# Splitting the load of the second x block over two queues, with half of V's weights queued behind the smaller part

## The chip, the cores and the metric

The kernel runs on one core of one Trainium2 chip. The metric is device time in microseconds (us) for one execution; lower is better. A time is the median of several runs. A core has five engines that each work through their own instructions in program order: TensorE (PE in the profile, with its weight loads as PEld), VectorE (DVE), ScalarE (ACT), GpSimd (POOL) and SyncE (SP). SP and ScalarE both issue DMA transfers, each into a queue of its own: q1 is SP's in the profile, q10 ScalarE's.

## The reference

The input x has 2048 rows of 640 values in bf16. Each row is normalized; the normalized x goes through windowed attention with 32 heads of 20 values, and through a gated feed-forward layer with 1536 hidden values. The output is x plus both:

```python
x = A_x
xn = _layernorm(x, axis=-1)
# A: 32 heads, a key is seen from its own row to 255 rows later
qkv = xn @ wqkv                      # 640 -> 3 * 640
p = softmax(mask(q @ k.T * Dh ** -0.5))
A = (p @ v) @ wo
# B: 640 -> 1536 -> 640
B = (sigmoid(xn @ w_gate) * (xn @ w_up)) @ w_down
return x + A + B
```

## The kernel before

The 2048 rows are worked on as four chunks of 512, each chunk as four blocks of 128 rows (128 is the number of partitions). For a chunk the kernel normalizes the blocks, transposes them to `xnT`, projects V (`project_v`, L321), then Q and K (`proj_block`, L294), and goes on to scores, exponentials, the product with V, the gate and up projections and the output. Work of later chunks is put between the attention steps of earlier ones by a list of fillers with costs, so that TensorE always has something to do.

The change is in the first microseconds, before any of that: chunk 0. Its order is written out by hand, and each engine runs its instructions in that order.

Loads. SP issues, one after another: block 0 of x (L171), block 1 (L171), block 3, block 2, the second column half of V's weights (L175), then the weights of Q and K (L165), the first half of the gate and up weights (L197) and two clears of scratch rows (L193). ScalarE issues one load: the first column half of V's weights, 128 partitions x 5 x 320 values, 400 KB (`load_v(0, nc.scalar)`, L179). A block of x is 160 KB, one row of 1280 bytes for each partition. A DMA counts up one of eight semaphores in turn, so that a later DMA that is given the same semaphore waits until the earlier one has landed.

Normalization of chunk 0. Block 0 has its statistics on VectorE (`ln_block`, L247 and L253). Blocks 1 and 3 have theirs on ScalarE: `mean_act` (L598) makes the mean, `root_act` (L603, L604) the variance and its root. The root for block 0 is ScalarE's as well (`root`, L588). The order is the one in which these lines are written:

```python
mv0 = ln_block(0, 0)
xn1, neg1 = mean_act(1)
r0 = root(mv0)
r1 = root_act(1, xn1, neg1)
norm(0, mv0, r0)
for lo, hi in ((0, 3), (3, DC)):
    transpose_rows(0, dve, lo, hi)
v00 = project_v(0, 0, 0)
norm_act(1, xn1, neg1, r1)
```

So on ScalarE the mean of block 1 comes ahead of the root of block 0. VectorE then normalizes block 0 (L592, L267), TensorE transposes it in five pieces (L274), VectorE copies these to `xnT` (L275), and TensorE makes the first product with V's first column half (L321). Block 1 follows in the same way (L608, L609), then both halves of V for blocks 0 to 3, and from there Q and K.

Before that, TensorE runs ten matmuls on constants (`pwarm`, L238), and ScalarE one SQRT on a constant (L234), which loads its function table.

Of the kernel before, what the change touches and what calls it, by code (L numbers as in the profile page):

```python
# [9 lines left out]
P = 128  # L10
# [97 lines left out]
def kernel(  # L108
# [11 lines left out]
    nc = tc.nc  # L120
    x2 = A_x.flatten_outer_dims()
    out2 = out.flatten_outer_dims()
    xr = x2.rearrange("(n p) d -> p n d", p=P)
# [25 lines left out]
    xc = {}  # L149
# [17 lines left out]

    xc[0] = xp.tile([P, SBC, D], BF16, name="xc")

    def load_rows(s, queue):  # L170
        queue.dma_start(out=xc[0][:, s, :], in_=xr[:, s, :])  # L171

    def load_v(hf, queue):
        a = 2 * D + hf * HALF
        queue.dma_start(out=wqkv[:, :, a:a + HALF], in_=wqkv_r[:, :, a:a + HALF])  # L175

    load_rows(0, nc.sync)
    load_rows(1, nc.sync)
    load_v(0, nc.scalar)  # L179
    load_rows(3, nc.sync)  # L180
    load_rows(2, nc.sync)
    load_v(1, nc.sync)
# [601 lines left out]
```

## Time and profile before

| what | value |
|---|---|
| median of 6 runs | 317.11 us (316.17 to 317.8) |
| the profiled execution, its own time | 317.8 us |
| its span, first to last instruction | 316.1 us |
| mean granted TensorE clock over the span | 0.987 |
| first product with V on TensorE (L321) | starts at 7.74 us |
| first product for Q (L294) | starts at 17.66 us |
| bytes that DMA moved in all | 35.71 MB, mean 113 GB/s |

The profile is that of one execution. Its times count from the start of the span. For each engine it lists the busy time and, before an instruction, the idle time and what ended it. "The chain that ended last" is followed back from the last instruction: at each step to what released it, or to the instruction before it on its engine. The granted clock is the share of TensorE's full clock that it was given. In the timeline, lines marked SPq or ACTq are the issues of DMAs by SP and ScalarE.

### The profile page before, as it was taken

The numbers are of one execution on the slowest core, as the hardware profiler recorded it, in microseconds if no ns is written. First come the engines' busy times: TensorE is split into PE (matmuls) and PEld (weight loads), VectorE is DVE, ScalarE is ACT, GpSimd is POOL, SyncE is SP. The second block draws the span as 40 slices with busy tenths as digits, with TensorE's granted clock in tenths as the row PEclk, the third lists the DMA queues.
The fourth block names the chain that finished last, engine by engine and source line by source line (L and its number), as shares of the span: only waits on it lengthen the run. The fifth ranks groups of instructions, "written<-read, shape, count | busy, mean of one in ns | idle before, by whom it ended". The sixth has DMA issues, their size and how long they took to land.

```text
span 316.1 us, 10548 instructions
## 1 busy us (share of the span) xinstructions
PE 308.6 (98%) x4663; PEld 176.7 (56%) x4663; DVE 159.6 (50%) x314; ACT 192.5 (61%) x178; POOL 155.7 (49%) x239
## 2 busy tenths in 40 slices
PE   5999999999999999999999999999999999999995
PEld 2555444556567665654557665654556675444774
DVE  2551746475695445269836245272632526372523
ACT  5424598688864747878574547867575647778000
POOL 3000286666783655748472736636372745556000
PEclk9599999999999999999999999999999999999999
DMA  7956899747554242640026222640000123000002
GB/s 252 372 170 233 264 379 249 221 126 209 177 91 106 64 129 84 198 155 2 4 41 88 66 72 79 206 144 2 2 3 2 62 66 108 0 4 0 5 21 63
DMA packets 37614, 35.71 MB, mean 113 GB/s; under 512 B 10272, under 2 KB 37024, under 8 KB 37536
## 3 DMA queue, kind: packets, MB, share of 16 engines
q1 hardware_dynamic: 36624, 34.51, 37.3%
q8 instruction: 36, 0.59, 0.7%
q10 hardware_dynamic: 944, 0.52, 0.5%
q14 instruction: 10, 0.08, 0.1%
HBM read 23.63 MB, written 10.26 MB: 107 GB/s over the span
## 4 chain that ended last, share of the span: by engine, by line
PE 96%; DMA 1%; DVE 1%; ACT 0%; issue 0%; SPq 0%; DVEq 0%
PE y L421 17%; PE pu L407 17%; PE pg L400 17%; PE pqk L294 14%; PE ps L471 9%; PE pv L321 8%; PE y L428 7%; PE acc L503 7%; DMA xc<-in_A_x_dram 1%; PE pt L274 1%; DVE xnT L275 0%; ACT xn L598 0%; DVE h L411 0%; DVE xn L267 0%; SPq L171 0%
## 5 line engine op out<-in xcount | busy, mean ns | idle before, releaser
L479 POOL TENSOR_SCALAR_AFFINE_SELECT pT<-pT 128x512 bf16<-128x512 bf16 (+2 forms) x192 | 147.2, 798 | 132.6 <-ACT pT L476 132.5
L476 ACT ACTIVATE pT<-ps 128x2048 bf16<-128x2048 f32 x76 | 142.7, 1878 | 64.3 <-PE ps L471 60.4
L411 DVE SCALAR_TENSOR_TENSOR h<-th,pu 128x512 bf16<-128x512 f32 x48 | 32.7, 683 | 60.3 <-PE pu L407 49.2
L407 PE MATMUL pu<-xnT,wu 128*128 128x512 bf16 x240 | 59.8, 380 | 0.0
L400 PE MATMUL pg<-xnT,wg 128*128 128x512 bf16 x240 | 59.8, 380 | 0.0
L421 PE MATMUL y<-wd,h 128*128 128x320 bf16 (+2 forms) x396 | 57.0, 296 | 0.0
L294 PE MATMUL pqk<-xnT,wqkv 128*128 128x512 bf16 x200 | 46.0, 381 | 0.0
L421 PEld LDWEIGHTS <-h 128*128 128x128 bf16 x396 | 36.5, 98 | 14.3
L403 ACT ACTIVATE th<-pg 128x512 f32<-128x512 f32 x48 | 28.6, 596 | 14.5 <-PE pg L400 14.2
L400 PEld LDWEIGHTS <-wg 128*128 128x128 bf16 x240 | 22.3, 98 | 25.3 <-issue 0.2
L407 PEld LDWEIGHTS <-wu 128*128 128x128 bf16 x240 | 21.9, 98 | 25.4 <-issue 0.6
L471 PEld LDWEIGHTS <-kT 20*64 20x64 bf16 x1856 | 20.6, 103 | 24.2 <-issue 21.9
L294 PEld LDWEIGHTS <-wqkv 128*128 128x128 bf16 x200 | 22.5, 119 | 18.0 <-issue 0.6
L471 PE MATMUL ps<-qT,kT 20*64 20x128 bf16 (+4 forms) x1856 | 32.5, 239 | 0.0
L513 DVE STREAM_TRANSPOSE t<-acc 128x512 f32<-128x512 f32 x32 | 22.0, 711 | 18.5 <-PE acc L503 18.2
L432 DVE SCALAR_TENSOR_TENSOR rows<-y,rows 128x320 bf16<-128x320 f32 x30 | 14.5, 490 | 33.2 <-PE y L428 33.1
L525 DVE TENSOR_TENSOR on<-t,rec 128x320 bf16<-128x320 f32 (+4 forms) x48 | 27.6, 574 | 1.1
L321 PE MATMUL pv<-wqkv,xnT 128*128 128x320 bf16 x160 | 26.0, 319 | 0.9 <-DVE xnT L275 0.9
L428 PE MATMUL y<-wo,oc 128*128 128x320 bf16 (+2 forms) x165 | 24.2, 295 | 0.0
L503 PE MATMUL acc<-pT,v 128*32 128x64 bf16 (+3 forms) x1376 | 23.2, 223 | 0.1
L503 PEld LDWEIGHTS <-v 128*32 128x32 bf16 x1376 | 18.6, 97 | 7.9 <-ACT pT L476 1.7
L321 PEld LDWEIGHTS <-xnT 128*128 128x128 bf16 x160 | 15.8, 103 | 8.5 <-DVE xnT L275 1.4
(44 smaller groups left out, 134.0 us busy)
## 6 DMA issues: line engine op xcount, KB each, us to landing
qT<-sq SPq DMA_DIRECT2D x7, 512.0 KB, 6.4
sq<-st SPq DMA_DIRECT2D x20, 128.0 KB, 2.6
sk<-st SPq DMA_DIRECT2D x20, 128.0 KB, 2.9
rows<-in_A_x_dram SPq DMA_DIRECT2D x15, 160.0 KB, 2.2
out_dram<-rows SPq DMA_DIRECT2D x15, 160.0 KB, 1.8
kT<-sk SPq DMA_DIRECT2D x4, 512.0 KB, 6.1
wg<-in_B_w_gate_dram SPq DMA_DIRECT2D x2, 960.0 KB
wu<-in_B_w_up_dram SPq DMA_DIRECT2D x2, 960.0 KB, 9.6
```

The source lines that it names most:

```text
L294: nc.tensor.matmul(ps, lhsT=wt[:, m, :], rhs=xnT[c][:, d, :], start=(d == 0), stop=(d == DC - 1))
L321: nc.tensor.matmul(ps[:, 0:HALF], lhsT=xnT[c][:, d, s * P:(s + 1) * P], rhs=wqkv[:, d, 2 * D + hf * HALF:2 * D + (hf + 1) * HALF], start=( ...
L400: nc.tensor.matmul(pg, lhsT=part(wg, d, f), rhs=xnT[c][:, d, :], start=(d == 0), stop=(d == DC - 1))
L403: nc.scalar.activation(out=th, in_=pg, func=TANH, scale=0.5)
L407: nc.tensor.matmul(pu, lhsT=part(wu, d, f), rhs=xnT[c][:, d, :], start=(d == 0), stop=(d == DC - 1))
L411: nc.vector.scalar_tensor_tensor(out=h, in0=th, scalar=1.0, in1=pu, op0=ADD, op1=MULT)
L421: nc.tensor.matmul(y[:, 0:cut[1] - cut[0]], lhsT=ht[c, f][:, s * P:(s + 1) * P], rhs=wd[:, f, cut[0]:cut[1]], start=(f == 0), stop=False)
L428: nc.tensor.matmul(y[:, 0:cut[1] - cut[0]], lhsT=oc[c, m][:, s * P:(s + 1) * P], rhs=wo[:, m, cut[0]:cut[1]], start=False, stop=(m == DC - 1))
L471: nc.tensor.matmul(ps[hf * U:(hf + 1) * U, i, col * U:(col + n) * U], lhsT=qk["k", kc, g // GH][32 * i:32 * i + DH, g % GH, key:key + U], ...
L476: nc.scalar.activation(out=pt[:, :, 0:CW], in_=ps, func=EXP, scale=SCALE)
L479: nc.gpsimd.affine_select(out=out, in_=in_, pattern=[[0, HG], [0, n], [sign, width]], compare_op=GE, fill=0.0, base=base, channel_multipli ...
L503: nc.tensor.matmul(acc[32 * i:32 * i + 32, q * U:(q + n) * U], lhsT=v[:, h * VW:h * VW + 32], rhs=pt[:, i, col * U:(col + n) * U], start=( ...
```

## The change

Block 1 of x is no longer loaded by one DMA. Its first 16 rows are loaded by ScalarE, which issues them ahead of V's first column half; SP loads the other 112 rows in the place where it loaded all 128. Everything else is as it was, in the same order on each engine. ScalarE thus issues two DMAs at the start where it issued one; SP issues as many as before. What reads block 1 (L598 and L609) waits for two DMAs where it waited for one. As the eight semaphores are given out in turn, each later DMA has the next one of that it had.

```diff
-    def load_rows(s, queue):
-        queue.dma_start(out=xc[0][:, s, :], in_=xr[:, s, :])
+    def load_rows(s, queue, a=0, b=P):
+        queue.dma_start(out=xc[0][a:b, s, :], in_=xr[a:b, s, :])
 
     def load_v(hf, queue):
         a = 2 * D + hf * HALF
         queue.dma_start(out=wqkv[:, :, a:a + HALF], in_=wqkv_r[:, :, a:a + HALF])
 
+    load_rows(1, nc.scalar, 0, 16)
     load_rows(0, nc.sync)
-    load_rows(1, nc.sync)
+    load_rows(1, nc.sync, 16, P)
     load_v(0, nc.scalar)
     load_rows(3, nc.sync)
     load_rows(2, nc.sync)
```

## The prediction

> **What bounds the kernel now.** I read the page first: busy shares, slices, the chain that ended last.
>
> ```profile
> PE 308.6 (98%) x4663; PEld 176.7 (56%) x4663; DVE 159.6 (50%) x314; ACT 192.5 (61%) x178; POOL 155.7 (49%) x239
> ...
> PEclk9599999999999999999999999999999999999999
> ...
> PE 96%; DMA 1%; DVE 1%; ACT 0%; issue 0%; SPq 0%; DVEq 0%
> ```
>
> TensorE is the end-setting engine nearly everywhere, so an edit of two loads can only matter where PE is not yet supplied: the first 18 us. There slice 2 also shows the one place where the granted clock was low. Next, the chain restricted to 0 to 19 us (start, length, what):
>
> ```profile
> 0.80 0.39 SPq L171
> 1.19 0.06 issue
> 1.25 3.92 DMA xc<-in_A_x_dram
> 5.17 0.02 issue
> 5.19 0.83 ACT xn L598 x2
> 6.02 0.19 ACT rstd L588
> ...
> 7.74 1.51 PE pv L321 x5
> ...
> 10.37 2.85 PE pv L321 x10
> ...
> 17.83 1.29 PE pqk L294 x6
> ```
>
> The chain passes through the *second* x block (issued at 1.25, landed at 5.17), although the first transposes need only the first block. ScalarE works in program order: mean_act(1) (L598) stands ahead of root(mv0) (L588), so block 0's reciprocal root waits for block 1. Block 0's own statistics had long been there: in the timeline L247 starts at 3.59 and L253 ends at 4.51 + 0.21 = 4.72.
>
> Why does 160 KB take 3.92 us? The DMA view by queue, for 3.25 to 4 us and then for 4.25 to 4.75 us (packets, MB, share of 16 engines; q1 is SP's queue, q10 ScalarE's):
>
> ```profile
> q10 hardware_dynamic: 421, 0.27, 112.1%
> q1 hardware_dynamic: 2, 0.00, 0.9%
> ```
>
> ```profile
> q1 hardware_dynamic: 173, 0.20, 109.2%
> q10 hardware_dynamic: 6, 0.00, 1.2%
> ```
>
> V's 400 KB half on q10 runs almost alone for that stretch, though block 1 stood in q1 since its issue at 1.25 to 1.67; only when V's half is through does q1 move again. Each queue's request was served whole: block 0, V's half, block 1. So block 1 waits for 400 KB.
>
> Last, the windows view (stretch, its length, PE, PEld, DVE, ACT and POOL busy, then granted clock, DMA share, GB/s), in stretches cut where the clock changes:
>
> ```profile
> 4.20:7.60 3.40, 1.06 (x8) 0.38 (x6) 1.37 (x6) 2.37 (x7) 0.00 (x0) 1.00 1.09 375
> 7.60:11.00 3.40, 2.67 (x13) 1.60 (x14) 2.32 (x9) 2.06 (x7) 0.00 (x0) 0.50 1.07 372
> 11.00:14.40 3.40, 3.40 (x18) 2.13 (x17) 1.46 (x4) 1.14 (x3) 0.00 (x0) 0.50 1.06 372
> 14.40:17.80 3.40, 3.40 (x29) 2.56 (x28) 0.99 (x2) 1.46 (x4) 0.00 (x0) 0.99 1.05 393
> ```
>
> After a stretch with PE busy 1.06 of 3.40 the clock was 0.50; after 2.67 of 3.40 it stayed; after a full one it was 1.00. At 0.50 ten L321 matmuls took 2.85 us (chain, 10.37), at 1.00 twenty took 2.72.
>
> **The change part by part.** *SP's second load loses 16 of 128 rows, and ScalarE gets one more issue.* SP keeps the same number of issues; of its times nothing moves (0.39 to 0.43 us each). ScalarE issues the 16 rows at 0.80 for about 0.40 (between SP's 0.39 and the 0.47 of V's half) and V's half at about 1.25 instead of 0.80. Behind it on ScalarE stand the table load (1.30, 1.28 us) and the warm-up SQRT (ended 3.00); both end about 0.45 later, 3.45, and the next instruction waits for block 1 at 4 us or later: hidden, by 0.6 us. A later block 1 only adds cover.
>
> *The order on the DMA engines* is the point. If the queues are again served request by request in turn, the order becomes block 0, the 16 rows, the other 112 rows, V's half. Block 1 then follows block 0 directly. DVE started on block 0 at 3.59; 160 KB at the 0.37 MB/us of these stretches is 0.44 us, so L598 could start at about 4.05 instead of 5.19. Bounds: not before 3.59 + 0.4, and not later than 5.19 if V's half still goes first. I take 4.07 (one more semaphore to wait for). Mean_act's 0.74 us then ends at 4.81, just behind block 0's statistics (4.72), so root(mv0) starts at 4.81 instead of 5.93: 1.12 us earlier. A landing still earlier by more than 0.1 us would gain nothing.
>
> In the Trainium skill, "DMA: Bandwidth & Descriptors", "Rules for kernel authors", speaks against this: two transfers to disjoint partition parts serialize on the same engines, so one 128-partition transfer is advised; by that rule the split itself buys nothing and the sum would be 0. The same page's "Queues, rings and completion order" says that each DMA engine goes round-robin between queue rows, a packet at a time; the 421 against 2 packets above are such turns, and by it the split gives the 1.12 us. I side with the packets, which show turns; no row shows the turn with a small request in ScalarE's queue.
>
> *V's half* lands later. In the timeline SP's L197 (whose issue waited for it) starts at 4.74; behind 160 KB more it lands at about 4.74 + 0.44 = 5.2. Its reader L321 starts at 7.74, or 6.62 when all is 1.12 earlier: still 1.4 us of cover. Without that cover each late us would stand before the first V matmul.
>
> *Blocks 3 and 2, V's second half, Q, K and gate weights*: the same bytes are ahead of each as before, so their landings stay. Needed 1.12 us or more earlier they still suffice: mean_act(3) read at 7.25. *Semaphores*: one more DMA shifts the reuse by one place, so SP's K load at 3.70 now waits for the 16 rows, the gate load at 4.74 for block 0 (landed by 3.59) instead of V's half, and the up load at 5.74 for V's half (5.2). All are met by then. ScalarE's L598 and DVE's L609 wait for two loads, some 0.02 us.
>
> *From the start of PE to the end.* Moved by 1.12, the transposes start at 5.83 (6.95 now), the first V group at 6.62 (7.74). If the clock falls at 7.61 and returns at 14.44 as now, these 5 matmuls run at full clock, 0.7 us instead of 1.51, and block 1's transposes (its xn ready at 8.43 - 1.12 = 7.31) are through by 7.64. DVE then has the half statistics of block 2 (0.48) until 7.79, the copy (0.49) until 8.30, and the second V group starts at 8.35, not 10.37. From there PE is never idle now until 17.83: 4.07 us at half clock (2.04 at full) and 3.39 at full, 5.43 in all. After: 8.35 to 14.44 gives 6.09 / 2 = 3.05, the other 2.38 end at 16.82. Gain 17.83 - 16.82 = 1.0 us; if the clock's boundaries moved along with the work it would be the plain 1.12. From 17.83 PE is the chain to its end, so the gain is carried through. The profiled execution took 317.8 us (316.1 of it span), hence 316.8; its time is the highest of the six runs, and from their median 317.11 the same 1.0 to 1.1 gives 316.0.
>
> **The rivals.** *R1, the clock is released earlier.* PE now works 0.61 (warm-up's end) + 0.45 (transposes) + 0.7 + 0.25, some 2.0 us of the stretch 4.2 to 7.6, against 1.06. Rows show that 1.06 lets the clock fall; nothing shows what 2.0 does. In 7.6 to 11.0 I get 2.7, like the 2.67 which did not release it, so the old pattern is likelier. If release comes at 11.03, 1.34 of the 5.43 is done by then and the rest ends at 15.12: 2.7 gained, 314.4. If the clock never falls, 8.35 + 5.43 = 13.78: 4.0 gained, 313.1. In the Trainium skill, "TensorE: Matmul & The Clock Gate", "What's actually happening", the activity window is free-running, 3,413 ns long, and the clock falls after an idle one; the 6.83 us at half clock here are two such windows. Whether 2.0 of 3.4 counts as idle it does not say, and a free phase would shift the boundaries from run to run.
>
> *R2, no gain: V's half still goes before the 112 rows.* ScalarE and SP issue at the same time (0.80 both). If the 16 rows reach an engine before block 0, the turns are 16 rows, block 0, V's half, 112 rows; one such engine of the 16 holds block 1 to 5.17. For: the start is a tie, and 0.40 against 0.39 decides. Against: in this trace block 0 preceded V's half although ScalarE's issue started no later. Price: L598 at 5.19 to 5.25, 317.1 to 317.2.
>
> *R3, slower: V's half comes too late.* If the engines take up all that SP has queued before ScalarE's second request, V's half lands with the Q part, which follows V's second half (landed 2.66 + 4.5 = 7.2) by 800 KB / 0.37 = 2.2 us: about 9.4, up to 9.9. L321 would start 1.7 to 2.1 us late, from the point on at which V's half lands after 7.74. PE's second V group then starts at 12.1 to 12.5, costing half of that before 14.44 and, with the gap moved into 11.0 to 14.4, possibly a further window at half clock: 318.0 to 319.7, taken as 318.2. For: nothing but the later issue. Against: q10 was served from 2.5 us on while q1 had block 1 queued.
>
> **How the numbers follow.** 0.3% is 0.95 us, so faster means below 316.16; that is about what a measurement of this kernel can tell from no change, and its six runs spread over 1.6. Forecast (block 1 early, clock as now) 0.45 at 316.0, of which a third may stay within 0.3%; R1 0.20; R2 0.27; R3 0.08. Faster 0.30 + 0.20 = 0.50; same 0.15 + 0.25 = 0.40; slower 0.10. The range runs from 313.8 (R1's early release with 0.6 to spare, the never-falling clock left out) to 317.6 (R2 with half a us of scatter); the forecast's own is 315.6 to 316.5.
>
> **What would show it.** Right: q1 carries the packets between 3.2 and 3.6 us and q10 after them; L598 starts near 4.1, L588 near 4.8, PE's first transposes near 5.8, and Q's first matmul (L294 before) near 16.8. The clock's row in 7.6 to 14.4 tells forecast from R1. L598 still at 5.2 is R2; an idle of L321 released by wqkv is R3. Wrong altogether: L598 early, but L588 waiting for DVE's L253 long after 4.8, or the time gained lost again before 36 us in a wait of PE for kT or qT.

## The result, and the profile after

The changed kernel took 314.14 us (median of 16 runs, 313.5 to 316.81) against 317.27 us for the kernel before (37 runs, 315.79 to 318.54). The ratio is 0.9919, 95% interval [0.9901, 0.9937]: 2.6 us faster. The profiled execution took 313.69 us, 312.0 of it span. All ratios here leave out executions that took over 1.5% longer than the fastest of the same kernel; there were two, 318.97 us with 13 warm-up matmuls and 318.40 us with V's half on SP.

The page of the changed kernel: engines' busy time, granted clock by slices, shares of the chain that ended last.

```profile
PE 306.3 (98%) x4663; PEld 175.3 (56%) x4663; DVE 159.6 (51%) x314; ACT 192.4 (62%) x178; POOL 155.7 (50%) x239
...
PEclk9999999999999999999999999999999999999999
...
PE 96%; DMA 1%; DVE 1%; ACT 0%; issue 0%; SPq 0%; DVEq 0%; ACTq 0%
```

The low second slice of the clock is gone. TensorE is busy 2.3 us less for the same 4663 matmuls. The chain restricted to the first 19 us (start, length, what; the code stands one line lower than before):

```profile
1.26 2.78 DMA xc<-in_A_x_dram
4.04 0.02 issue
4.06 0.02 ACTq L599
4.08 0.05 issue
4.13 0.83 ACT xn L599 x2
4.96 0.19 ACT rstd L589
...
6.74 0.85 PE pv L322 x5
...
8.53 1.53 PE pv L322 x10
...
14.01 5.18 PE pqk L295 x24
```

Block 1 is through at 4.04 instead of 5.17, and the chain still goes through it. From there, however, the chain shortens a second time: five V matmuls take 0.85 us instead of 1.51, ten take 1.53 instead of 2.85, and Q starts on the chain at 14.01 instead of 17.83. That is 3.8 us, of which only 1.1 are the landing.

The order of the transfers, in the DMA view by queue for 2.5 to 3 us, then for 3.75 to 4.25 us (packets, MB, share of 16 engines):

```profile
q1 hardware_dynamic: 120, 0.13, 92.2%
q10 hardware_dynamic: 15, 0.01, 5.8%
```

```profile
q10 hardware_dynamic: 285, 0.18, 114.0%
```

q1's two blocks now go first and V's half after them; q1 stands still only behind block 1. The windows, cut as before (stretch, length, busy time of PE, PEld, DVE, ACT, POOL, then granted clock, DMA share, GB/s):

```profile
4.20:7.60 3.40, 2.44 (x15) 1.02 (x14) 2.08 (x9) 3.33 (x9) 0.00 (x0) 1.00 1.10 371
7.60:11.00 3.40, 2.81 (x28) 2.07 (x27) 2.82 (x9) 2.09 (x7) 0.00 (x0) 1.00 1.06 373
11.00:14.40 3.40, 3.40 (x29) 2.46 (x27) 1.33 (x3) 1.87 (x4) 0.00 (x0) 1.00 1.06 373
```

In the second and third of these stretches the clock was 0.50 before. (The clock's record begins with its first release, here at 6.06. Ahead of it the view shows 1.00, although the warm-up matmuls follow each other at 0.43 us, half the speed of the 0.22 us that matmuls of the same 512 columns take from 14.01 on; so a late first release does not show in the mean clock.)

### The profile page after: what moved, and what is told of

Same layout as the page of the kernel before. It is cut to its first block, busy times and chain, and to the rows that moved or that the text cites. A ratio compares the mean times of both kernels' runs of the same rounds, so it can differ in the third digit from the quotient of the medians.

```text
span 312.0 us, 10550 instructions
## 1 busy us (share of the span) xinstructions
PE 306.3 (98%) x4663; PEld 175.3 (56%) x4663; DVE 159.6 (51%) x314; ACT 192.4 (62%) x178; POOL 155.7 (50%) x239
## 4 chain that ended last, share of the span: by engine, by line
PE 96%; DMA 1%; DVE 1%; ACT 0%; issue 0%; SPq 0%; DVEq 0%; ACTq 0%
PE y L422 17%; PE pu L408 17%; PE pg L401 17%; PE pqk L295 14%; PE ps L472 9%; PE pv L322 7%; PE y L429 7%; PE acc L504 7%; DMA xc<-in_A_x_dram 1%; PE pt L275 0%; DVE xnT L276 0%; ACT xn L599 0%; DVE h L412 0%; DVE xn L268 0%; SPq L171 0%
## 5 line engine op out<-in xcount | busy, mean ns | idle before, releaser
L322 PE MATMUL pv<-wqkv,xnT 128*128 128x320 bf16 x160 | 23.6, 300 | 0.9 <-DVE xnT L276 0.9
L322 PEld LDWEIGHTS <-xnT 128*128 128x128 bf16 x160 | 14.9, 98 | 7.3 <-DVE xnT L276 1.3
```

What stands on the lines that cost most here:

```text
L322: nc.tensor.matmul(ps[:, 0:HALF], lhsT=xnT[c][:, d, s * P:(s + 1) * P], rhs=wqkv[:, d, 2 * D + hf * HALF:2 * D + (hf + 1) * HALF], start=( ...
```

## The experiments

All twelve were timed against the kernel before, and the ratios are to it. T1 is the theory that the landing gives about 1.1 us and the clock the rest, because TensorE idles less between its warm-up and its first transposes; T2 that all of it is the landing.

### The kernel before, once more

No edit.

> The kernel before, once more, for the clock of many executions. Theory T1 (block 1's earlier landing gives about 1.1 us, and the rest of the gain is TensorE's clock, which falls in the kernel before because TensorE idles some 2 us between its warm-up and its first transposes): nearly every execution shows a mean clock below 0.995 or a late first release, and no execution comes under 315. Theory T2 (all of the gain is the earlier landing and its consequences; the clock of the profiled execution of before was chance): several executions show a clock of 1.0 and times no better than the others. Ratio 1.000 in both.

Ratio 0.9996 [0.9976, 1.0016], 12 runs from 315.81 to 318.89. With the other runs of the kernel before in these comparisons there are 82 executions with their mean clock. In 69 of them it is below 0.996 (one stretch of 3.41 us at half clock costs 0.005 over the span); the other 13 have no recorded fall but are no faster, 317.04 to 318.49. None is under 315. The largest group, 36 executions at 0.995, has a median of 316.28; the 28 at 0.987 and 0.989, which is two stretches, have 317.56 and 318.60, and the profiled one is among them. So the clock differs from run to run, but almost always costs something. The windows of this profile, cut at its own changes of the clock, show it falling after one release and coming back sooner than in the profile shown first:

```profile
4.60:8.01 3.41, 1.31 (x11) 0.63 (x10) 1.45 (x6) 2.94 (x9) 0.00 (x0) 1.00 1.05 350
8.01:11.42 3.41, 2.83 (x15) 1.59 (x14) 2.72 (x9) 1.83 (x6) 0.00 (x0) 0.50 1.07 376
11.42:14.84 3.41, 3.41 (x33) 2.62 (x32) 1.09 (x4) 1.62 (x4) 0.00 (x0) 1.00 1.06 374
```

### The clock alone: more warm-up, loads untouched

```diff
-    for n in (6, 4):
+    for n in (6, 4, 6):
```

> The kernel before with 16 warm-up matmuls where it had 10, loads untouched. T1: L598 still starts at 5.2 and the transposes at 6.95, but the idle time before them is gone and the clock stays at 1.0 through 17 us; from the first transposes to the first Q matmul it then takes 8.0 us as in the changed kernel (5.88 to 13.85), so Q starts near 14.9 and the ratio to before is 0.991 to 0.994. T2: the warm-up changes nothing that is waited for, Q starts at 17.7, ratio 0.999 to 1.003.

Ratio 0.9940 [0.9915, 0.9965], none of 9 executions with a fall. The chain in its profile:

```profile
4.99 0.83 ACT xn L598 x2
...
7.53 0.85 PE pv L321 x5
...
9.32 1.53 PE pv L321 x10
...
14.81 0.22 PE pqk L294
```

Block 1 is about as late as ever (L598 at 4.99; 5.19 and 5.01 in the two profiles of before), yet the V matmuls run at full clock and Q is 3 us earlier than in the profile of before. T2 is out: 1.9 us are to be had without touching a load.

### The clock alone: the same warm-up, later

```diff
-            nc.tensor.matmul(ps, lhsT=ones[:, 0:P], rhs=ones, start=(k == 0), stop=(k == n - 1))
+            nc.tensor.matmul(ps, lhsT=ident, rhs=ones, start=(k == 0), stop=(k == n - 1))
```

> The kernel before with its 10 warm-up matmuls taking the identity as weights, which GpSimd finishes at 2.7 us: as many as before, but they start near 2.7 instead of 0.84 and end near 6.5 to 7, where the transposes begin; L598 still at 5.0 to 5.2. If the idle time between warm-up and work is what costs the clock, the clock does not fall again after its first release, Q starts near 15, ratio 0.991 to 0.996. If the number of warm-up matmuls is what counts (16 against 10), the ratio is 0.998 to 1.003.

Ratio 0.9943 [0.9922, 0.9965], none of 12 with a fall. TensorE's timeline (start, length, what, the idle time before it and its releaser):

```profile
2.73 4.45 PE L238 MATMUL pwarm<-const-bfloat16-1.0,ident 128*128 128x512 bf16 x10 [2.73 <-POOL ident masks.py:199]
6.97 0.74 PE L274 MATMUL pt<-ident,xn 128*128 128x128 bf16 x5
7.95 0.94 PE L321 MATMUL pv<-wqkv,xnT 128*128 128x320 bf16 x5 [0.24 <-DVE xnT L275]
```

Ten matmuls as in the kernel before, but they end where the transposes begin, and the gain is that of sixteen. The first release comes late in this profile, at 8.16, yet the clock holds after it. So what costs the clock in the kernel before is the idle time between warm-up and work, and ten matmuls are enough. The number is not without effect, as the next run shows.

### The landing with the old idle time: less warm-up

```diff
-    for n in (6, 4):
+    for n in (4, 3):
```

This is an edit of the changed kernel.

> The changed kernel with 7 warm-up matmuls where it had 10, so that TensorE idles 2.0 us before its first transposes, as in the kernel before. T1: L599 starts at 4.1 and the transposes at 5.9 as in the changed kernel, but the clock is at 0.5 for 3 to 7 us of the first 15, and only the 1.0 to 1.1 us of the earlier landing is left: ratio to before 0.996 to 0.998. T2: as the changed kernel, ratio 0.990 to 0.993.

Ratio 1.0003 [0.9982, 1.0025]: neither theory's number. TensorE's timeline:

```profile
0.84 3.15 PE L239 MATMUL pwarm<-const-bfloat16-1.0 128*128 128x512 bf16 x7 [0.84 <-PEq L769]
6.00 0.72 PE L275 MATMUL pt<-ident,xn 128*128 128x128 bf16 x5 [2.01 <-DVE xn L268]
6.95 1.51 PE L322 MATMUL pv<-wqkv,xnT 128*128 128x320 bf16 x5 [0.24 <-DVE xnT L276]
...
9.58 2.85 PE L322 MATMUL pv<-wqkv,xnT 128*128 128x320 bf16 x10 [0.58 <-DVE xnT L276]
```

The landing is early (transposes at 6.00), but the V matmuls run at half clock, and the record of the clock has its first release only at 13.03. With seven warm-ups nothing released it at the start, which is worse than what I meant to copy. (The mean clock is 1.000 in 11 of the 12 executions all the same, this one among them, as it does not count what comes before the first release.) The run refutes T2 a second time, the early landing being there and the gain not; it does not price the landing by itself.

### The changed kernel with more warm-up, and once more as it is

```diff
-    for n in (6, 4):
+    for n in (6, 4, 3):
```

> The changed kernel with 13 warm-up matmuls, which fill the 1 us that TensorE still idles before its first transposes. T1: fewer executions lose the clock or get it late, those above 315 go, ratio to before 0.987 to 0.990. T2: as the changed kernel, 0.990 to 0.993, or slower where the warm-up runs past 5.9 us.

> The changed kernel once more: ratio to before 0.990 to 0.993; L599 near 4.1; in most executions no fall of the clock, in one of four a late first release or one fall, 315 to 317.

With 13 warm-ups: 0.9927 [0.9904, 0.9950], so no further gain, against T1's number. Where the clock's first release is late, 13 matmuls at 0.43 us last until 6.4 and hold up the transposes, which are ready at 5.9; that this is the cause was not tried. In the profile of this run, an execution of 318.97 us, TensorE stood idle for 2.42 us until up weights (`wu`) landed at 44.13, and the clock fell at 44.62. A low mean clock can thus come from a later place too. The changed kernel again: 0.9939 [0.9912, 0.9966]. Of its 29 executions in both comparisons 5 have a fall (mean clock 0.995), and 5 others took 316.48 to 316.81 without one. The latter fit a late first release, which the mean clock doesn't show; neither profile of the changed kernel caught one, so this is not shown.

The landing can be priced at the same clock in two ways, both rough. The executions with one fallen stretch have a median of 316.28 before (36 of them) and 315.23 after (5, from 314.99 to 316.4): 1.05 us. Those with no fall recorded have 314.14 in the changed kernel (24 of 29), and 315.19 and 315.25 in the two runs above that touch only the warm-up of the kernel before: 1.05 to 1.1 us.

### What decides the fall

In every profile the changes of the clock are whole stretches of 3.41 us apart, and the first of them lies elsewhere each time. So one can ask how busy PE was in the first stretch after the release. In the changed kernel with block 0's root first (its diff is below) the clock fell after the first line and came back after the second; in the repeated changed kernel it held after the line in the second fence (columns as above):

```profile
5.11:8.53 3.41, 1.90 (x16) 0.97 (x15) 2.40 (x8) 3.31 (x9) 0.00 (x0) 1.00 1.09 373
8.53:11.94 3.41, 3.19 (x16) 2.04 (x17) 1.76 (x7) 1.76 (x7) 0.00 (x0) 0.50 1.07 367
```

```profile
4.72:8.13 3.41, 1.99 (x17) 0.97 (x15) 2.09 (x7) 3.35 (x10) 0.00 (x0) 1.00 1.08 376
```

In this first stretch PE busy 1.06 (before), 1.31 (before again) and 1.90 of 3.41 us were followed by a fall; 1.99 and everything above was not. The changed kernel's two profiles have 2.49 and 1.99, so it sits at or above the edge, and the kernel before far below it. The edge holds for this kind of stretch only: in the last stretch with work at the kernel's end, 1.40 and 1.43 were followed by a fall, but 1.47 and 1.60 were not. So busy time is not quite what decides. It counts for each group of matmuls a modelled end of some 0.16 us (five V matmuls alone show 0.85, within a row of twenty 0.68), and a first stretch has three or four such groups where the end has one. An estimate that counts only the spacing within a row (in the changed kernel's chain twenty V matmuls take 2.72 us and five transposes 0.28) makes 1.24 us of the 1.90 and 1.27 of the 1.43 that fell, 1.31 of the 1.47 and some 1.4 of the 1.99 that held. One edge near 1.3 us would fit these; nothing here tries it. In the other direction 2.70 at half clock did not release it (7.61 to 11.03 in the first profile), 2.80 did:

```profile
2.64:6.06 3.41, 2.80 (x9) 0.77 (x8) 1.71 (x5) 2.46 (x8) 0.76 (x11) 1.00 1.03 323
6.06:9.47 3.41, 2.49 (x22) 1.55 (x21) 2.89 (x10) 2.80 (x9) 0.00 (x0) 1.00 1.08 379
```

This is the changed kernel's profile, at the stretch that ends in its first release and the one behind it, in which the clock held.

### Any small request, and one queue

First: block 1 whole on SP, and ahead of V's half on ScalarE the same 16 rows to a place that is overwritten later and read by nobody before that.

```diff
+    nc.scalar.dma_start(out=wd[0:16, 0, :], in_=xr[0:16, 1, :])
     load_rows(0, nc.sync)
     load_rows(1, nc.sync)
     load_v(0, nc.scalar)
```

> The kernel before, with block 1 whole on SP, and ahead of V's half on ScalarE a load of the same 16 rows to a place that nobody reads. If the queues are served request by request in turn, the small request takes V's turn, block 1 comes before V's half, L599 starts near 4.1, ratio 0.990 to 0.994 as in the changed kernel. If the split matters by itself (fewer rows on SP), L599 starts at 4.5 or later and the ratio is above 0.996.

Ratio 0.9936 [0.9906, 0.9966], with the chain's

```profile
4.05 0.83 ACT xn L599 x2
4.88 0.19 ACT rstd L589
```

The split has no part in it: 16 rows that nobody needs do the same. Whether they take a turn of ScalarE's queue, or only hold back the issue of V's half by 0.45 us, until block 1's stands in SP's, these runs do not tell apart.

Second: nothing on ScalarE's queue.

```diff
     load_rows(1, nc.sync)
-    load_v(0, nc.scalar)
+    load_v(0, nc.sync)
```

> The kernel before with V's first half issued by SP, third, behind block 0 and block 1 whole: no split, and nothing on ScalarE's queue. If all that counts is that block 1 is served before V's half (T1's first part), L598 starts near 4.1, the transposes near 5.9, the clock holds as in the changed kernel, ratio to before 0.990 to 0.994. If two queues are needed, because one queue is slower to feed the engines at the start, L598 starts later than 4.5 and the ratio is above 0.996.

> V's first half on SP, third, once more, now beside the changed kernel on the same chip. If one queue in the right order is better than the changed kernel's two, by the 0.4 to 0.5 us by which block 1 landed earlier, the ratio to before is 0.988 to 0.990 and 0.001 to 0.002 below the changed kernel's. If the difference was chance, both 0.990 to 0.993.

Ratios 0.9888 [0.9860, 0.9917] and 0.9895 [0.9864, 0.9926], the latter beside the changed kernel's 0.9939 on the same chip. The chain of the first:

```profile
1.26 2.33 DMA xc<-in_A_x_dram
3.58 0.02 issue
3.61 0.83 ACT xn L598 x2
...
6.31 1.07 PE pv L321 x5
```

Block 1 is through at 3.58, another 0.46 us earlier than in the changed kernel. Of the 12 executions of both runs one shows a fall (318.40 us, mean clock 0.995). The version is faster than the kernel before, and both of its ratios lie below both of the changed kernel's (0.9919 and 0.9939); but the intervals overlap, so that it beats the changed kernel is likely and not shown. In the profile of the repeat, L598 starts at 3.61 as well, but the chain now comes through V's second column half, which landed at 8.84: the next load to look at.

### The order on ScalarE

```diff
-    xn1, neg1 = mean_act(1)
     r0 = root(mv0)
+    xn1, neg1 = mean_act(1)
```

In the kernel before, in the changed one, and with V's half on SP:

> The kernel before with the root of block 0 ahead of the mean of block 1 on ScalarE, loads untouched. If block 1's landing only counts because ScalarE's order puts block 0 behind it, L588 starts near 4.75 and the transposes near 5.8 although L598 still starts at 5.2; the second V group, which needs block 1, starts near 8.9 (8.53 in the changed kernel), the clock holds in most executions, ratio 0.990 to 0.995. If block 1 itself is what is waited for, the transposes come earlier but the second V group stays near 10, ratio 0.997 to 1.000.

> The changed kernel with the same exchange on ScalarE: the root of block 0 no longer waits for block 1's mean (L599, 0.74 us), only for its own statistics (L254, ended 4.47). Transposes near 5.5 instead of 5.88, second V group near 8.2 instead of 8.53, idle before the transposes shorter still: ratio to before 0.988 to 0.991. If the mean of block 1 is delayed as much as the root gains, as the changed kernel: 0.991 to 0.993.

> V's first half on SP, third, and the root of block 0 ahead of the mean of block 1. Block 1 lands at 3.6 with V on SP, block 0's statistics end near 4.2: the root can start 0.15 us earlier, and the mean of block 1 (0.74 us) now ends before the second V group needs it. If they add, ratio 0.987 to 0.989; if block 1's mean, now behind the root, delays the second V group, 0.989 to 0.992.

With no load touched at all, this exchange of two lines gives 0.9919 [0.9894, 0.9944]. ScalarE's timeline in it:

```profile
4.37 0.29 ACT L588 ACTIVATE rstd<-mv,eps 128x1 f32<-128x1 f32 x1 [1.36 <-DVE mv L253]
5.10 0.74 ACT L598 ACTIVATE xn<-xc 128x640 bf16<-128x640 bf16 x1 [0.43 <-DMA xc<-in_A_x_dram]
```

Block 1 is still late (5.10), block 0 no longer waits for it, and the transposes start at 5.40. TensorE then idles 0.74 us for block 1's, and no fall is recorded in any of the 6 executions. On top of the changed kernel the exchange gives 0.9911 [0.9881, 0.9941], and with V on SP 0.9900 [0.9869, 0.9931]: no gain that can be told. There block 1 lands before block 0's statistics are done, so the root had little to wait for.

## Why the prediction was wrong

*The landing* was right in each step that counts: L599 at 4.13 (4.07 forecast), L589 at 4.87 (4.81), first transposes at 5.88 (5.83), first V group 6.74 (6.62), second V group 8.53 (8.35). V's half was not late: L322 at 6.74 was released by VectorE's copy. Its price by the steps was 1.0 to 1.1 us; executions at the same clock give 1.05 to 1.1. One step was off without effect: the warm-up SQRT ended at 3.22 and not 3.45, since in the kernel before it had waited 0.21 us for `eps`.

*The step that failed* is "If the clock falls at 7.61 and returns at 14.44 as now". I took the clock of one execution as fixed in time and put the other case, R1, at 0.20. The right sentence stood in R1: some 2.0 us of work in the stretch, against 1.06 that let the clock fall. What I lacked was the edge, which for this stretch lies between 1.90 and 1.99 of 3.41, right where my sum of 2.0 was. What the runs showed in its place: of 29 executions 24 have no recorded fall (five of these were slow in another way, perhaps by a late release), and the forecast's case was the exception. Without touching a load, the clock alone gave 1.9 us.

*The size of the other case* was right too: never falling, Q's start on the chain was to be 13.78 and was 14.01, and 4.0 us off the profiled 317.8 is 313.8 against 313.69 for the profiled execution after. But I took those 4.0 off the median, which gave 313.1, and left the case out of the range. That 314.14 still lies inside the range is luck: its lower end, 313.8, stood for a release at 11.03, which did not happen. The median of the kernel before contains many executions that lose 3.41 us at half clock (41 of 82) and not 6.83 like the profiled one (28 of 82), which is of the slower kind. The gain is therefore 2.6 us (1.9 in the repeat) and not 4.0: about 1.05 of landing, and the rest, 0.9 to 1.5, of clock. The clock alone gave 1.9 with 16 warm-ups, where no execution showed a fall.

*The rivals.* R2 (V's half still first) and R3 (V's half too late) did not happen; the packets went in the order forecast, though sooner (between 3.25 and 3.75 us q10 already had 137 of 178). The 421 against 2 packets of the prediction are not turns packet by packet: they show one queue served for a whole request, which is what the sum used. The advice weighed there, not to split a transfer over disjoint partitions (the Trainium skill, "DMA: Bandwidth & Descriptors", "Rules for kernel authors"), is borne out in one respect: the split itself gained nothing, and whole blocks in one queue did at least as well.

## What to carry to other kernels

At the start of a kernel, look at three things together: which load the first work waits for, which instruction stands ahead of that work on its engine, and how long TensorE idles between warm-up and work. Here each of three one-line edits (the order of loads, the order of two ScalarE instructions, the time of the warm-up) gave 0.6 to 1.1%. Two of them together gave no more that could be told, which fits if most of each is the same clock. And where the clock changes in a profile, one execution is not the kernel: read the mean clock of many runs before you take a time off the median.

## What was not expected of the hardware

The clock's changes lie a whole number of 3.41 us stretches apart, at a phase that differs from execution to execution (first release at 4.20, 4.60, 6.06 and, with seven warm-ups, 13.03 us), and each fall or release follows the stretch that ends there. That the phase is free is also what the Trainium skill says ("TensorE: Matmul & The Clock Gate", "What's actually happening"). The edges in the first microseconds, by the profile's busy time of PE: a fall after 1.90 of 3.41 us or less, none after 1.99 or more; a release after 2.80 or more, none after 2.70. At the kernel's end the edge of the fall lay lower, between 1.43 and 1.47.

With V's half on SP and nothing on ScalarE's queue, block 0 too was there earlier: VectorE began at 3.04, 3.09 and 3.15 us in three profiles, against 3.29 to 3.59 in most profiles with a load on ScalarE's queue (3.20 in one). Why was not tried.
